# A new order of the first loads, pair 0 scaled on one engine, and two moved instructions in a fused attention and mixer kernel

## The chip, the cores and the metric

The kernel runs on one core of one Trainium2 chip. A core has five engines, each with its own queue of instructions that it works off in order: TensorE (PE in the profile) for matrix products, VectorE (DVE), ScalarE (ACT), GpSimd (POOL), and SyncE (SP), which here only issues DMA transfers. Engines wait for one another through semaphores. The metric is the time of one execution on the device in microseconds (us); lower is better.

## The reference

Two stages follow one another. The first is cosine attention over 8 batches and 12 heads, sequence 448, head size 64:

```
q_n = q / (norm(q) + 1e-06);  k_n = k / (norm(k) + 1e-06)
attn = softmax(q_n @ k_n.T / tau)          # tau = 0.1
x = attn @ v                               # heads side by side: (8, 448, 768)
```

The second is an MLP mixer on x, without normalisation:

```
h = maximum(x.T @ w_tok1, 0) @ w_tok2      # w_tok1 448x256, w_tok2 256x448
u = x + h.T
out = u + maximum(u @ w_ch1, 0) @ w_ch2    # w_ch1 768x1536, w_ch2 1536x768
```

Inputs and output are 32-bit floats. The kernel multiplies in 16-bit floats.

## The kernel before, in words

The heads are taken in pairs: 6 pairs in each of 8 batches, 48 in all. The sequence of 448 is split into 4 chunks of 112 rows. One pair passes through these steps:

- `load`: three DMA copies (q, k, v; 224 KB each) from SyncE. There are five buffers of each, so that pair i + 5 is loaded while pair i is at work.
- `squares` (GpSimd; ScalarE for pairs 0 and 1), `norm_sum` (VectorE), `norm_root` (ScalarE: logarithm, then exponential of half of it), `norm_rec` (VectorE): they give one over the norm.
- `normalize`: q and k are multiplied by it and written in 16 bits. GpSimd does it, except that for pair 0 VectorE takes half of k.
- `tpose_pe`: eight TensorE transposes and a copy out of PSUM by VectorE (for pair 0 by ScalarE, q and k apart). From pair 14 on a DMA transposes instead.
- `score`: TensorE, four tiles of 112x896, with two PSUM buffers between them; `expo`: ScalarE takes the exponential of each.
- `v_cast`: V is cast to 16 bits, by ScalarE or VectorE, as a list of pairs says.
- `pv`: 32 matmuls give output and row sums; VectorE divides and writes x.

Everything runs in an order written out by hand; no scheduler moves anything. `opening(i)` issues the instructions of slots 0 to 12, `slot(i)` those of the later ones. In slot i the scores of pair i, the output of pair i - 1 and the preparation of pairs i + 1 to i + 3 stand side by side. `fill()` puts in matmuls of the mixer of an earlier batch, from slot 7 on (`spread` sets how many).

The mixer of batch 0 starts inside the opening slots. In slots 2 to 6 it goes pair by pair: `tok1_pair` (first token weight, TensorE, then a relu on ScalarE), `tok2_pair` (second token weight), and `u_pair`, an addition on VectorE done twice: once into 16 bits, from which a DMA transposes a piece of uT, and once into 32 bits. Slot 6 handles two pairs, 4 and 5, and so has four additions.

The weights of the token stage come in 32 bits: `w1_load` (seven pieces and one repeated piece) and `w2_load` on SyncE. VectorE casts w1 in slot 1 (`w1_cast`, two halves of a 128x1280 tile); ScalarE casts w2 in slots 1 and 2 (`w2_cast`). The last 64 rows of w1 are kept twice, once in partitions 0 to 63 with zeros beside them, and once in partitions 64 to 127 (fifth column block), for batches with an odd number. The channel weights come through GpSimd's queue in slots 1, 3, 5, 7 and 9 to 11 (`wc1_job`, `wc2_job`).

The order of the first loads on SyncE (lines 439 to 452) is: q, k of pair 0; q, k of pair 1; v of 0; q, k of 2; v of 1; q, k of 3; w1; w2; q, k of 4; v of 2, 3, 4.

Of the kernel before, what the change touches and what calls it, by code (L numbers as in the profile page):

```python
# [9 lines left out]
FP32 = mybir.dt.float32  # L10
FP16 = mybir.dt.float16
AF = mybir.ActivationFunctionType
ALU = mybir.AluOpType
# [5 lines left out]
def _bcast_free(ap: bass.AP, n: int) -> bass.AP:  # L19
    return bass.AP(tensor=ap.tensor, offset=ap.offset, ap=list(ap.ap) + [[0, n]])  # L20
# [3 lines left out]
def kernel(  # L24
# [19 lines left out]
    nc = tc.nc  # L44

    B, H, S, E = q.shape
# [51 lines left out]
    def ident():  # L98
        nc.gpsimd.memset(id16[:], 0.0)
        nc.gpsimd.affine_select(out=id16[:], in_=id16[:], compare_op=ALU.not_equal,  # L100
                                fill=1.0, base=0, pattern=[[-1, 128]], channel_multiplier=1)
        for t in v16s:
            nc.gpsimd.memset(t[:, :, E:E + 1], 1.0)
        st = mix.tile([128, 5, T], FP32, name="w1s", tag="u32", bufs=2)
        stage["w1"] = st
        nc.gpsimd.memset(st[64:128, 3, :], 0.0)
        nc.gpsimd.memset(st[0:64, 4, :], 0.0)

    def w1_load(n):
        st = stage["w1"]  # L110
        rows = moe_w_tok1.rearrange("(p c) t -> c p t", c=NCH)
        if n < 3:
            for f, m in f_segments(128 * n, 128 * n + 128):
                c, p = f // P, f % P
                nc.sync.dma_start(out=st[f - 128 * n:f - 128 * n + m, n, :],
                                  in_=rows[c, p:p + m, :])
        else:
            nc.sync.dma_start(out=st[0:64, 3, :], in_=rows[3, P - 64:P, :])
            nc.sync.dma_start(out=st[64:128, 4, :], in_=rows[3, P - 64:P, :])

    def w2_load():
        st = mix.tile([128, TT, S], FP32, name="w2s", tag="u32", bufs=2)
# [3 lines left out]
    def recast(out, in_):  # L126

        nc.vector.tensor_reduce(out=out, in_=bass.AP(tensor=in_.tensor, offset=in_.offset,  # L128
                                                     ap=list(in_.ap) + [[1, 1]]),
                                axis=AXX.X, op=ALU.max)  # L130

    def w1_cast(z):
        a, o = (t[:].rearrange("p n t -> p (n t)") for t in (stage["w1"], w1t))
        h = 5 * T // 2
        recast(o[:, z * h:(z + 1) * h], a[:, z * h:(z + 1) * h])

    def w2_cast(tt):
        nc.scalar.copy(out=w2t[:, tt, :].rearrange("k (c p) -> k c p", c=NCH),
# [21 lines left out]
    def load(i, names="qkv"):  # L160
        b, pj = pairs[i]
        for nm in names:
            t = ld.tile([P, 2, NCH, E], FP32, name=f"{nm}l", tag=f"{nm}l")
            nc.sync.dma_start(
                out=t[:].rearrange("p g c e -> p g (c e)"),
                in_=src[nm][b, 2 * pj:2 * pj + 2].rearrange("g (p c) e -> p g (c e)", c=NCH))
            st_[i][nm] = t

    def squares(i, act=""):
        s = st_[i]  # L170
        s["sq"] = att.tile([P, 2, 2 * NCH, E], FP32, name="sq", tag="sq", bufs=2)
        for j, nm in enumerate("qk"):
            a = s[nm][:].rearrange("p g c e -> p (g c) e")
            if nm in act:
                nc.scalar.activation(out=s["sq"][:, j], in_=a, func=AF.Square)  # L175
            else:
                nc.gpsimd.tensor_mul(out=s["sq"][:, j], in0=a, in1=a)  # L177

    def small(i, nm):
        if nm not in st_[i]:  # L180
            st_[i][nm] = att.tile([P, 2, 2 * NCH], FP32, name=nm, tag=nm)
        return st_[i][nm]
# [3 lines left out]
    def norm_sum(i, j=BOTH):  # L186
        nc.vector.tensor_reduce(out=small(i, "ssq")[:, j], in_=st_[i]["sq"][:, j], axis=AXX.X,  # L187
                                op=ALU.add)

    def norm_root(i, j=BOTH):  # L190
        nc.scalar.activation(out=small(i, "ln")[:, j], in_=small(i, "ssq")[:, j], func=AF.Ln)  # L191
        nc.scalar.activation(out=nns[i % 3][:, j, :, 0], in_=small(i, "ln")[:, j], func=AF.Exp,
                             scale=0.5)

    def norm_rec(i, j=BOTH):

        nc.vector.tensor_reduce(out=small(i, "nre")[:, j], in_=nns[i % 3][:, j], axis=AXX.X,
                                op=ALU.add)
        nc.vector.reciprocal(out=small(i, "rn")[:, j], in_=small(i, "nre")[:, j])  # L199

    def normalize(i, vec):
        s = st_[i]
        t = att.tile([P, 2, NCH, 2, E], FP16, name="qkn", tag="qkn")
        for j, nm in enumerate("qk"):
            for g in ((0, 1) if vec and j else (BOTH,)):
                eng = nc.vector if g == 1 else nc.gpsimd
                rn = small(i, "rn")[:, j].rearrange("p (g c) -> p g c", g=2)[:, g]
                o = t[:, j, :, g, :]
                if g == BOTH:
                    o = o.rearrange("p c g e -> p g c e")  # L210
                eng.tensor_tensor(out=o, in0=s[nm][:, g], in1=_bcast_free(rn, E), op=ALU.mult)  # L211
        s["qkn"] = t

    def v_cast(i, act):
# [47 lines left out]
    def expo(i, c):  # L262
        s = st_[i]
        nc.scalar.activation(out=s["p"][:, c], in_=s["pS"][c][:, :, 0:S], func=AF.Exp,  # L264
                             scale=inv_tau)
# [174 lines left out]
    eps()  # L440
    load(1, "qk")
    ident()
    load(0, "v")
    load(2, "qk")
    load(1, "v")
    load(3, "qk")
    for n in range(4):
        w1_load(n)
    w2_load()
    load(4, "qk")  # L450
    for n in (2, 3, 4):
        load(n, "v")
    squares(0, act="qk")
    for j in range(2):
        norm_sum(0, j)
        norm_root(0, j)
    for j in range(2):
        norm_rec(0, j)
    squares(1, act="qk")
    normalize(0, True)  # L460
    tpose_pe(0, act=True)
    norm_sum(1)
    norm_root(1)
    norm_rec(1)
    squares(2)

    wide = {**{i: partial(wc1_job, n) for n, i in enumerate((1, 3, 5, 7))},
# [1 line left out]

    def opening(i):  # L470

        normalize(i + 1, False)
        score(i, 0)
        norm_sum(i + 2)
        expo(i, 0)
        expo(i, 1)
        if not i:
            v_cast(0, True)
        norm_root(i + 2)
        v_cast(i + 1, i in (0, 2, 3, 4, 5))  # L480
        squares(i + 3)
        if i in wide:
            wide[i]()
        fill()
        if i >= 1:
            pv(i - 1, 0)
            pv(i - 1, 1)
        norm_rec(i + 2)
        if i in (1, 2):
            w2_cast(i - 1)  # L490
        r_, u_, add = first[0] if first else (None,) * 3
        done = [i - 2] if 2 <= i <= NPAIR else []
        if done:
            r_(i - 2)
        fill()
        score(i, 1)
        expo(i, 2)
        expo(i, 3)
        tpose_pe(i + 1)
        if i == NPAIR:  # L500
            r_(i - 1)
            done.append(i - 1)
        for pj in done:
            u_(pj)
        for half in (True, False):
            for pj in done:
                add(pj, half)
        if i == 1:
            w1_cast(0)
            w1_cast(1)  # L510
        fill()
        fill()
        fill()
# [98 lines left out]
```

## Time and profile before

| | before |
|---|---|
| median of 3 runs | 413.39 us (412.63 to 414.4) |
| the profiled execution | 413.88 us |
| its span, first to last instruction | 411.5 us |
| TensorE busy | 383.9 us, 93% of the span |
| VectorE busy | 233.9 us, 57% |
| ScalarE busy | 262.1 us, 64% |
| GpSimd busy | 198.2 us, 48% |
| moved by DMA | 63.63 MB, mean 155 GB/s |

The span lies 2.4 us below the profiled execution's own time; that rest lies outside the first and last instruction. Times below are from the start of the span. The profile shows, for each engine, when an instruction started, how long it took, and what ended the idle time before it; a chain of waits, followed back from the last instruction; and the clock granted to TensorE, as a share of its full speed.

### The profile page before, as it was taken

The numbers are of one execution on the slowest core, as the hardware profiler recorded it, in microseconds if no ns is written. First come the engines' busy times: TensorE is split into PE (matmuls) and PEld (weight loads), VectorE is DVE, ScalarE is ACT, GpSimd is POOL, SyncE is SP. The second block draws the span as 40 slices with busy tenths as digits, with TensorE's granted clock in tenths as the row PEclk, the third lists the DMA queues.
The fourth block names the chain that finished last, engine by engine and source line by source line (L and its number), as shares of the span: only waits on it lengthen the run. The fifth ranks groups of instructions, "written<-read, shape, count | busy, mean of one in ns | idle before, by whom it ended". The sixth has DMA issues, their size and how long they took to land.

```text
span 411.5 us, 9002 instructions
## 1 busy us (share of the span) xinstructions
PE 383.9 (93%) x3592; PEld 220.6 (54%) x3592; DVE 233.9 (57%) x530; ACT 262.1 (64%) x452; POOL 198.2 (48%) x207
## 2 busy tenths in 40 slices
PE   2768789899999999999999999999999999999996
PEld 1456556556445556555545556555545556655453
DVE  4499978748634776548643676448643683152022
ACT  6879869876576666765677666775677665522400
POOL 4979969934743564634653464635563430000000
PEclk9989989999999999999999999999999999999999
DMA  8899999966974588649876488539963253027013
GB/s 212 239 247 216 221 252 234 248 139 140 238 155 109 139 181 198 160 75 184 219 178 150 124 196 198 151 84 199 209 166 91 61 120 101 2 43 149 0 43 112
DMA packets 97385, 63.63 MB, mean 155 GB/s; under 512 B 57536, under 2 KB 93888, under 8 KB 97344
## 3 DMA queue, kind: packets, MB, share of 16 engines
q1 hardware_dynamic: 94032, 58.20, 60.1%
q0 software_dynamic: 3184, 4.72, 6.7%
q8 instruction: 28, 0.46, 0.5%
q10 hardware_dynamic: 128, 0.15, 0.1%
q14 instruction: 13, 0.11, 0.1%
HBM read 43.45 MB, written 11.01 MB: 132 GB/s over the span
## 4 chain that ended last, share of the span: by engine, by line
PE 78%; DVE 11%; DMA 3%; ACT 3%; POOL 2%; issue 1%; DVEq 0%; POOLq 0%
PE pG L375 27%; PE pF L384 25%; PE pO L278 9%; PE pS L257 9%; PE pR L309 5%; PE pU L322 3%; DVE ssq L187 2%; DVE x L285 2%; ACT pE L264 2%; DMA uT<-u 1%; DVE qkT L246 1%; DMA kl<-in_k_dram 1%; POOL qkn L211 1%; DVE u L366 1%; DVE u L331 1%; POOL sq L177 1%
## 5 line engine op out<-in xcount | busy, mean ns | idle before, releaser
L264 ACT ACTIVATE pE<-pS 112x896 f16<-112x896 f32 x192 | 164.9, 914 | 39.5 <-PE pS L257 38.8
L375 PE MATMUL pG<-uT,wc1t 128*128 128x384 f16 (+1 forms) x576 | 121.4, 355 | 0.3 <-DMA uT<-u 0.3
L384 PE MATMUL pF<-wc2t,gT 128*128 128x384 f16 x672 | 116.6, 326 | 0.2
L211 POOL TENSOR_TENSOR qkn<-ql,rn 112x512 f16<-112x512 f32 x48 | 50.1, 1044 | 137.7 <-DVE rn L199 122.4
L384 PEld LDWEIGHTS <-gT 128*128 128x128 f16 x672 | 63.6, 98 | 47.0 <-issue 7.3
L377 ACT ACTIVATE gT<-pG 128x384 f16<-128x384 f32 (+1 forms) x96 | 52.6, 548 | 45.9 <-PE pG L375 45.1
L375 PEld LDWEIGHTS <-wc1t 128*128 128x128 f16 x576 | 51.7, 98 | 51.9 <-issue 11.5
L388 DVE TENSOR_TENSOR u<-pF,u 128x384 f32<-128x384 f32 x56 | 31.1, 556 | 78.5 <-PE pF L384 78.0
L257 PE MATMUL pS<-qkT 64*112 64x448 f16 x384 | 60.2, 384 | 13.2 <-DVE qkT L246 10.3
L278 PEld LDWEIGHTS <-pE 112*128 112x128 f16 x1536 | 60.8, 100 | 15.9 <-issue 5.4
L278 PE MATMUL pO<-v,pE 112*128 112x65 f16 x1536 | 64.8, 196 | 0.0
L187 DVE TENSOR_REDUCE ssq<-sq 112x16 f32<-112x1024 f32 (+1 forms) x49 | 58.3, 1192 | 5.5 <-ACT sq L175 3.7
L284 DVE RECIPROCAL rec<-pO 128x6 f32<-128x6 f32 x96 | 17.5, 182 | 77.1 <-PE pO L278 76.1
L211 POOL TENSOR_TENSOR qkn<-kl,rn 112x512 f16<-112x512 f32 (+1 forms) x48 | 49.8, 1038 | 0.0
L177 POOL TENSOR_TENSOR sq<-ql 112x512 f32<-112x512 f32 x46 | 48.8, 1061 | 1.6 <-ACT qkT L244 1.2
L177 POOL TENSOR_TENSOR sq<-kl 112x512 f32<-112x512 f32 x46 | 48.5, 1053 | 0.2 <-DMA kl<-in_k_dram 0.2
L285 DVE TENSOR_TENSOR x<-pO,rec 128x384 f16<-128x384 f32 x96 | 40.9, 426 | 3.3
L257 PEld LDWEIGHTS <-qkT 64*112 64x112 f16 x384 | 19.0, 127 | 39.1 <-issue 22.8
L128 DVE TENSOR_REDUCE v<-vl 112x512 f16<-112x512 f32 x39 | 24.9, 639 | 3.4 <-DMA vl<-in_v_dram 3.4
L331 DVE TENSOR_TENSOR u<-pU,x 128x384 f32<-128x384 f32 x50 | 25.4, 545 | 0.1
L337 ACT CAST u<-u 128x768 f16<-128x768 f32 x14 | 11.6, 832 | 20.9 <-DVE u L331 20.9
L191 ACT ACTIVATE ln<-ssq 112x16 f32<-112x16 f32 (+1 forms) x49 | 10.9, 223 | 17.7 <-DVE ssq L187 17.5
(41 smaller groups left out, 181.9 us busy)
## 6 DMA issues: line engine op xcount, KB each, us to landing
ql<-in_q_dram SPq DMA_DIRECT2D x48, 224.0 KB, 3.8
kl<-in_k_dram SPq DMA_DIRECT2D x48, 224.0 KB, 4.0
vl<-in_v_dram SPq DMA_DIRECT2D x48, 224.0 KB, 4.2
out_dram<-u SPq DMA_DIRECT2D x8, 336.0 KB, 3.5
wc1t<-in_moe_w_ch_dram POOLq DMA_DIRECT2D x4, 576.0 KB, 7.5
wc2t<-in_moe_w_ch_dram POOLq DMA_DIRECT2D x3, 768.0 KB, 10.3
out_dram<-u SPq DMA_DIRECT2D x8, 288.0 KB, 3.8
out_dram<-u SPq DMA_DIRECT2D x7, 240.0 KB, 3.1
```

The costliest lines, as they stand in the source:

```text
L177: nc.gpsimd.tensor_mul(out=s["sq"][:, j], in0=a, in1=a)
L187: nc.vector.tensor_reduce(out=small(i, "ssq")[:, j], in_=st_[i]["sq"][:, j], axis=AXX.X, op=ALU.add)
L211: eng.tensor_tensor(out=o, in0=s[nm][:, g], in1=_bcast_free(rn, E), op=ALU.mult)
L257: nc.tensor.matmul(pS[:, h, 0:S], s["T"][64 * h:64 * h + 64, 1, c * P:(c + 1) * P], s["T"][64 * h:64 * h + 64, 0, :], start=True, stop=True)
L264: nc.scalar.activation(out=s["p"][:, c], in_=s["pS"][c][:, :, 0:S], func=AF.Exp, scale=inv_tau)
L278: nc.tensor.matmul(pO[:, n, h, :], s["p"][:, c, h, c0:c0 + 128], s["v16"][:, NCH * h + c, 0:E + 1], start=(c == 0), stop=(c == NCH - 1))
L285: nc.vector.tensor_tensor(out=xt[hp:hp + nr, t0:t0 + len(ts), d0:d0 + 2 * E].rearrange("p t (h e) -> p t h e", h=2), in0=pO[m0:128, :, :, ...
L331: nc.vector.tensor_tensor(out=u32[:, i - t0, cols], in0=pU[:], in1=xt[:, i, cols], op=ALU.add)
L375: nc.tensor.matmul(pG[:], wc1t[:, dt, ct * 128:(ct + 1) * 128], uT[:, dt, :], start=(dt == 0), stop=(dt == DT - 1))
L377: nc.scalar.activation(out=gT[:, ct, :], in_=pG[:], func=AF.Relu)
L384: nc.tensor.matmul(pF[:], gT[:, ct, (i - t0) * 128:(i - t0 + 1) * 128], wc2t[:, ct, dh * DH:(dh + 1) * DH], start=(ct == 0), stop=(ct == C ...
L388: nc.vector.tensor_tensor(out=o, in0=pF[:], in1=o, op=ALU.add)
```

## The change

- The first loads are issued in another order: q, k of pairs 0, 1, 2; v of 0; q, k of 3; v of 1 and 2; q, k of 4; w1; w2; v of 3 and 4.
- The repeated piece of w1 isn't loaded any more. The zeros are written by GpSimd into the 16-bit tile, VectorE casts 768 columns of 128 partitions and 256 columns of 64 partitions in slot 1, and in slot 8 copies the 16-bit rows from partitions 0 to 63 to partitions 64 to 127.
- Pair 0 is scaled on VectorE alone, q and k whole.
- Pair 1: q is squared on ScalarE, k on GpSimd, and the norms are summed in two halves. Its root and its reciprocal are issued in slot 0 after the first exponential, and its scaling after these.
- The 32-bit addition of pair 5 is issued in slot 7, after the copy of pair 8's transposes, not in slot 6.
- V of pair 8 is cast in slot 7 by ScalarE, not by VectorE.

```
@@ ident
-        st = mix.tile([128, 5, T], FP32, name="w1s", tag="u32", bufs=2)
+        st = mix.tile([128, 4, T], FP32, name="w1s", tag="u32", bufs=2)
         stage["w1"] = st
-        nc.gpsimd.memset(st[64:128, 3, :], 0.0)
-        nc.gpsimd.memset(st[0:64, 4, :], 0.0)
+        nc.gpsimd.memset(w1t[64:128, 3, :], 0.0)
+        nc.gpsimd.memset(w1t[0:64, 4, :], 0.0)
@@ w1_load
             nc.sync.dma_start(out=st[0:64, 3, :], in_=rows[3, P - 64:P, :])
-            nc.sync.dma_start(out=st[64:128, 4, :], in_=rows[3, P - 64:P, :])
@@ w1_cast
-        a, o = (t[:].rearrange("p n t -> p (n t)") for t in (stage["w1"], w1t))
-        h = 5 * T // 2
-        recast(o[:, z * h:(z + 1) * h], a[:, z * h:(z + 1) * h])
+        if z < 2:
+            p, n = (slice(0, 64), slice(3, 4)) if z else (slice(0, 128), slice(0, 3))
+            recast(w1t[p, n, :], stage["w1"][p, n, :])
+        else:
+            recast(w1t[64:128, 4, :], w1t[0:64, 3, :])
@@ normalize
-            for g in ((0, 1) if vec and j else (BOTH,)):
-                eng = nc.vector if g == 1 else nc.gpsimd
...
+            eng = nc.vector if vec else nc.gpsimd
+            rn = small(i, "rn")[:, j].rearrange("p (g c) -> p g c", g=2)
+            eng.tensor_tensor(out=t[:, j].rearrange("p c g e -> p g c e"), in0=s[nm][:],
+                              in1=_bcast_free(rn, E), op=ALU.mult)
@@ the first loads and steps
     load(1, "qk")
     ident()
+    load(2, "qk")
     load(0, "v")
-    load(2, "qk")
+    load(3, "qk")
     load(1, "v")
-    load(3, "qk")
+    load(2, "v")
+    load(4, "qk")
     for n in range(4):
         w1_load(n)
     w2_load()
-    load(4, "qk")
-    for n in (2, 3, 4):
-        load(n, "v")
+    load(3, "v")
+    load(4, "v")
...
-    squares(1, act="qk")
+    squares(1, act="q", names="q")
+    squares(1, names="k")
     normalize(0, True)
     tpose_pe(0, act=True)
-    norm_sum(1)
-    norm_root(1)
-    norm_rec(1)
+    for j in range(2):
+        norm_sum(1, j)
     squares(2)
@@ opening
-        normalize(i + 1, False)
-        score(i, 0)
-        norm_sum(i + 2)
-        expo(i, 0)
+        if i:
+            normalize(i + 1, False)
+            score(i, 0)
+            norm_sum(i + 2)
+            expo(i, 0)
+        else:
+            score(0, 0)
+            expo(0, 0)
+            norm_root(1)
+            norm_rec(1)
+            normalize(1, False)
+            norm_sum(2)
         expo(i, 1)
...
-        v_cast(i + 1, i in (0, 2, 3, 4, 5))
+        v_cast(i + 1, i in (0, 2, 3, 4, 5, 7))
...
         for pj in done:
             u_(pj)
+        if i == NPAIR + 1:
+            first[0][2](NPAIR - 1, False)
         for half in (True, False):
             for pj in done:
-                add(pj, half)
+                if half or pj != NPAIR - 1:
+                    add(pj, half)
+        if i == NPAIR + 2:
+            w1_cast(2)
```

More of the change, by code (lines that the diff above doesn't have):

```diff
@@ L167, in load, with squares @@
             st_[i][nm] = t
-    def squares(i, act=""):
+    def squares(i, act="", names="qk"):
         s = st_[i]
-        s["sq"] = att.tile([P, 2, 2 * NCH, E], FP32, name="sq", tag="sq", bufs=2)
-        for j, nm in enumerate("qk"):
+        if "sq" not in s:
+            s["sq"] = att.tile([P, 2, 2 * NCH, E], FP32, name="sq", tag="sq", bufs=2)
+        for nm in names:
+            j = "qk".index(nm)
             a = s[nm][:].rearrange("p g c e -> p (g c) e")
@@ L204, in normalize @@
         for j, nm in enumerate("qk"):
-            for g in ((0, 1) if vec and j else (BOTH,)):
-                eng = nc.vector if g == 1 else nc.gpsimd
[L207 to L211, printed above, removed]
+            eng = nc.vector if vec else nc.gpsimd
+            rn = small(i, "rn")[:, j].rearrange("p (g c) -> p g c", g=2)
+            eng.tensor_tensor(out=t[:, j].rearrange("p c g e -> p g c e"), in0=s[nm][:],
+                              in1=_bcast_free(rn, E), op=ALU.mult)
         s["qkn"] = t
```

## The prediction

> **What bounds the kernel now.** I read the page's slices first, then the chain of waits, then each engine in order of time over the first 62 us, where the diff acts, and the clock.
>
> ```profile
> PE   2768789899999999999999999999999999999996
> DVE  4499978748634776548643676448643683152022
> PEclk9989989999999999999999999999999999999999
> ...
> PE 78%; DVE 11%; DMA 3%; ACT 3%; POOL 2%; issue 1%; DVEq 0%; POOLq 0%
> ```
>
> A slice is 10.3 us. TensorE (PE) is full from slice 9 on, so there a microsecond is only won by starting earlier. In the first eight slices it isn't full, and the granted clock dips in slices 3 and 6. The order of instructions on TensorE is the same in both kernels, so time won before 60 us should reach the end nearly whole. What holds it up early:
>
> ```profile
> 15.01 1.22 DVE L187 TENSOR_REDUCE ssq<-sq 112x16 f32<-112x1024 f32 x1 [0.75 <-POOL sq L177]
> 19.62 0.69 DVE L128 TENSOR_REDUCE v<-vl 112x512 f16<-112x512 f32 x1 [3.39 <-DMA vl<-in_v_dram]
> ...
> 22.07 0.62 DVE L246 COPY qkT<-pT 128x896 f16<-128x896 f16 x1
> ```
>
> ```profile
> 22.75 0.99 PE L257 MATMUL pS<-qkT 64*112 64x448 f16 x4 [3.56 <-DVE qkT L246]
> ...
> 53.60 2.10 PE L375 MATMUL pG<-uT,wc1t 128*128 128x384 f16 x6
> ```
>
> (Start, us taken, engine, line, operation, and the idle time before it.) VectorE (DVE) waits 3.4 us for V of pair 2; the copy of pair 2's transposes is queued behind that, and TensorE then stands 3.6 us. The second place is slot 7: VectorE runs without a gap to 52.9, TensorE idles 2.65 us for pair 8's copy, and the six matmuls after that take 2.1 us, against 1.14 at 58.04. The clock says why:
>
> ```profile
> 19.15:22.56 3.41, 0.04 (x1) 1.00 1.12 270
> 22.56:25.97 3.41, 3.22 (x42) 0.50 1.13 256
> 25.97:29.39 3.42, 2.49 (x27) 1.00 1.12 257
> ...
> 49.86:53.28 3.42, 0.77 (x12) 1.00 0.93 203
> 53.28:56.69 3.41, 3.41 (x32) 0.50 1.11 226
> ```
>
> (Stretch, TensorE busy us, clock.) After a stretch of 3.41 us with 0.04 or 0.77 us of work, the next 3.41 us have half the clock; after 2.49 us it stays full. At the very start the column reads 1.00, but four score matmuls take 0.99 us until 22.75 and 0.59 from 26.22: TensorE runs at half pace there too.
>
> **The loads.** The first ten loads run in one file: k of pair 0 lands at 4.1, q1 6.2, k1 7.1, the tenth (k of pair 3) 7.2 us after its issue at 5.18, so at 12.4. From the third to the tenth that is 0.89 us each. SP's eleventh issue, at 6.18, is at the landing of the third copy: each waits for the one eight before it. In the new order pair 2's q and k are fifth and sixth (7.9, 8.8), V of pair 0 9.7, V of pair 1 tenth (12.4), V of pair 2 eleventh (13.3, not 19.6), pair 4's k thirteenth (15.1; before, issue 14.04 plus 4.5 = 18.5). VectorE's 3.4 us wait goes.
>
> What is late next is the channel weight w2. It becomes the twenty-first issue and waits for the thirteenth landing, 15.1. Before it took
>
> ```profile
> w2s<-in_moe_w_tok_dram SPq DMA_DIRECT2D x1, 448.0 KB, 3.6
> ```
>
> so it lands at 18.7 (before 12.9 + 3.6 = 16.5). w1 is in by about 16.5 (its last part issues at 14.2 and takes 2.1 to 2.4) and is wanted near 19.5. ScalarE (ACT) casts w2 in slot 1 ahead of two exponentials.
>
> **Slot 0.** Before, GpSimd scales q in 5.97 to 7.01 and half of k to 7.76, VectorE the other half:
>
> ```profile
> 5.97 1.04 POOL L211 TENSOR_TENSOR qkn<-ql,rn 112x512 f16<-112x512 f32 x1 [3.73 <-DVE rn L199]
> 6.97 0.79 POOL L211 TENSOR_TENSOR qkn<-kl,rn 112x256 f16<-112x256 f32 x1
> ```
>
> VectorE's half (256 elements) ran 6.46 to 7.29, 0.83 us; only 0.28 of it lies after GpSimd's q. GpSimd's half took 0.79, not half of 1.04. I read both as one waiting for the other: 0.28 us for 256 elements, some 0.6 for 512. (128x384 products elsewhere take 0.56, which gives 0.75 as upper end without a wait; 2 x 0.83 = 1.67 if the wait were its own pace.) New: q 6.46 to 7.06, k to 7.66, scores at 8.85, not 9.0: 0.15 gained. But GpSimd now squares pair 1's k, which lands at 7.06, just when VectorE goes from q to k. If GpSimd slips in between, k is 1.04 later. I take it that VectorE keeps on.
>
> The Trainium skill, "SBUF — State Buffer", section "🔬 SBUF: two separate sides", says that a GpSimd operation and a VectorE operation with two SBUF inputs exclude each other for the whole instruction; that agrees with the pair of rows, and it speaks against this change, as it puts a GpSimd square among the VectorE products: with GpSimd in between, the sum below would be about 0.5 less.
>
> Pair 1's root now stands behind the first exponential, 9.5 to 10.4 on ScalarE, so its reciprocal is ready at 11.3, not 9.98; GpSimd was busy squaring pair 2 until 10.98 anyway, so its scaling moves from 10.94 to 11.3. All of slot 0 behind that is 0.3 us later: pair 2's root, V of pair 1, exponentials, pair 3's root, w2 cast at 17.25, not 16.96.
>
> **Slots 1 and 2.** ScalarE waits 17.25 to 18.7, casts (0.98), pair 1's last exponentials end at 21.3 (before 19.7). VectorE meanwhile casts V of pair 2 at 16.6, does pair 0's output (17.2 to 18.5), the reciprocal, and pair 2's copy at 19.5, not 22.07. The w1 casts shrink from 2 x 640 columns (22.61 to 24.07, 1.14 ns a column) to 768 + 256: 1.17 for 1.46, 0.3 gained. So pair 2's exponentials start on ScalarE at 21.3, not 23.41: 2.1; the train behind them (root, V cast, second w2 cast, relu) reaches its last exponentials at 25.05, not 27.36: 2.3; and VectorE's next block, which waits for them, comes at 28.0, not 30.43: **2.4 us**. Pair 5's loads for that stretch land about where they did (w2 2.2 later, but V of 2 and q, k of 4 no longer in between). From there to slot 6 ScalarE and VectorE repeat unchanged at 4.44 us a slot.
>
> Bounds: if w2 takes 2.1 us, the quickest weight copy, ScalarE doesn't wait and VectorE sets 3.0; if 6.6, the slowest (w1's first), ScalarE waits 4.45 and the 2.4 becomes -0.6. I take 3.6, its own row. If the clock is halved through slot 2 (TensorE is idle from about 19.5 to 21.7 but for two matmul pairs), the scores, transposes and pU there take about twice as long and the gain is 1.3.
>
> **Slots 6 to 8.** Slot 6 loses one of four additions (0.47) and slot 7 the V cast (0.59) ahead of pair 8's copy: it ends at 51.85 in old time, not 52.91. **1.06 us**, TensorE's idle time falls from 2.65 to 1.6. ScalarE takes the cast (0.6) after pair 9's root, which comes 0.47 earlier; its last exponential ends near 52.1, just before the scores need it. The addition returns behind pair 8's copy (0.5), ahead of a 2.36 us idle: nothing, and with a full clock VectorE would still be free at 54.05 for an output at 54.3. The pieces for the six matmuls land at 52.3 (issue 49.0 + 3.3), just ahead of 52.5. Slot 8 gains a 64x256 cast, 0.29 + 0.06; pair 10's copy has 0.34 of idle before it: nothing, at most 0.35. The two GpSimd memsets (0.3 each) only change their target.
>
> If TensorE's shorter pause no longer halves the clock, the six matmuls take 1.14 (1.0 less) and the 32 after them 1.19, not 1.69: **1.5 us** more. Its busy share would be about half a stretch; the rows show 0.23 tripping and 0.73 not. Unknown between, and where the stretch falls is chance. The Trainium skill, "TensorE: Matmul & The Clock Gate", section "🔬 Part 1: The HAM clock gate (the "warmup" mystery)", asks for a whole idle window; by it both pauses are too short and the sum would be 5.0, though this trace shows 0.77 us of work not sufficing.
>
> **Sum.** One of the two slow stretches stays, the other goes: 2.4 + 1.06 = 3.5 (slot 8 slow), or 1.3 + 1.06 + 1.5 = 3.9 (slot 2 slow). I take 3.6. The profiled execution took 413.88 (span 411.5 and 2.4 around it), 0.5 above the median 413.39: 410.3 beside the profile, 409.8 beside the median; I say **410.0**.
>
> **Rivals.**
> - Both slow stretches go: 2.4 + 1.06 + 1.5 = 5.0, 408.4 to 408.9. For: both pauses are shorter than those that tripped. Against: at the start busy shares of 0.66 (12.32 to 15.73) and 0.73 (8.91 to 12.32) did not bring the full pace.
> - Both stay, or GpSimd slips in (1.04, of which ScalarE's wait for w2 hides about half): 1.3 + 1.06 = 2.4, less 0.5: 1.9 to 2.4, 411.0 to 411.5.
> - The wait for w2 takes the place of that for V: each late microsecond past 18.7 costs one. At a landing of 20.5 or later the early gain is under 0.6 and the whole 0.6 to 1.7: about 412.3. For: six small w1 pieces ahead of it each hold one of eight places. Against: it only waits for the thirteenth landing.
> - Slower than before: the same wait at its upper bound. With w2 at 21.7 the sum is -0.6 + 1.06 = +0.5; past 22.2 it turns to a loss, past 24.3 the loss exceeds 0.5%, 415.5.
>
> **Chances.** 0.42, 0.22, 0.22, 0.10, 0.04 in that order. 0.5% (2.07 us) is about what can be told from no change: faster means under 411.3, so the first two, half the third: 0.75; the rest of the third and the fourth, 0.21, same; 0.04 slower. The range runs from 407.8 (both stretches gone, 408.4, and the 0.6 that an early w2 adds) to 412.4 (w2 in V's place); it leaves out about 0.15.
>
> **What would show it.** V's wait of 3.4 gone on VectorE; ScalarE idle about 1.5 us before the first w2 cast; VectorE's two scalings of about 0.6 each, scores at 8.85; the output block of slot 3 at about 28; one halved stretch, not two; TensorE's pause before pair 8's scores about 1.6. I am wrong if w2 lands after 20, if both stretches stay, or if TensorE waits later for something that the earlier start doesn't bring forward (a transposed piece, a load).

## The result and the profile after

The changed kernel takes 410.59 us (median of 16 executions), the kernel before 413.37 (median of 16 beside it). The ratio is 0.9926, 95% interval 0.9909 to 0.9943: 0.74% faster. The profiled execution took 411.94 us with a span of 410.1 us; before it was 413.88 with 411.5. So of the 1.94 us between the two profiled executions 1.4 lie in the span and 0.54 outside it. One of the 16 executions, 416.08 us at a mean clock of 0.982, lies over 1.5% above the fastest and isn't in the ratio; with it the changed kernel's mean is 411.07 us, without it 410.74.

The page of the changed kernel, its slices and the shares of its chain:

```profile
PE   1779789889999999999999999999999999999996
DVE  5688998648534766558644766548643673152022
PEclk9978999999999999999999999999999999999999
...
PE 77%; DVE 9%; DMA 6%; POOL 4%; issue 1%; ACT 1%; SPq 1%; DVEq 0%; POOLq 0%
```

TensorE is as full from slice 10 on as before; slice 9 fell from 9 to 8, and the third wait below lies in it. The clock dips once, in slices 3 and 4, and no longer in slice 6. VectorE's part of the chain fell and that of DMA doubled. The two places that the prediction started from, VectorE first and TensorE after it (start, us, engine, line, operation, idle time before it):

```profile
16.75 1.22 DVE L190 TENSOR_REDUCE ssq<-sq 112x16 f32<-112x1024 f32 x1 [0.75 <-POOL sq L180]
17.89 0.68 DVE L127 TENSOR_REDUCE v<-vl 112x512 f16<-112x512 f32 x1
...
20.37 0.62 DVE L246 COPY qkT<-pT 128x896 f16<-128x896 f16 x1
```

```profile
21.05 0.69 PE L257 MATMUL pS<-qkT 64*112 64x448 f16 x4 [0.77 <-DVE qkT L246]
...
52.02 0.63 PE L257 MATMUL pS<-qkT 64*112 64x448 f16 x4 [1.59 <-DVE qkT L246]
52.58 1.15 PE L375 MATMUL pG<-uT,wc1t 128*128 128x384 f16 x6
```

V of pair 2 is cast without a wait. TensorE's pauses fell from 3.56 to 0.77 us and from 2.65 to 1.59, and the six matmuls in slot 8 run at full pace (1.15, not 2.10). But the ends do not add up so simply. Three things came in between.

First, slot 0 is later than before. VectorE scales pair 0, GpSimd squares pair 1's k:

```profile
6.84 0.64 DVE L210 TENSOR_TENSOR qkn<-ql,rn 112x512 f16<-112x512 f32 x1
7.40 1.53 DVE L210 TENSOR_TENSOR qkn<-kl,rn 112x512 f16<-112x512 f32 x1
```

```profile
7.17 1.21 POOL L180 TENSOR_TENSOR sq<-kl 112x512 f32<-112x512 f32 x1 [4.94 <-DMA kl<-in_k_dram]
8.34 1.48 POOL L180 TENSOR_TENSOR sq<-ql 112x512 f32<-112x512 f32 x1
```

The k scaling takes 1.53 us against 0.64 for q of the same size, and the GpSimd squares around it 1.21 and 1.48 against 1.04 elsewhere. GpSimd's first square started at 7.17, ahead of VectorE's k scaling at 7.40, and VectorE finished after it; the second square, at 8.34, finished after VectorE. Pair 1's copy starts at 15.37, before at 13.63.

Second, a half-clock stretch now comes in slot 3. In stretches of 3.41 us (length, TensorE busy us with the number of matmuls, clock, then two columns on DMA):

```profile
22.88:26.29 3.41, 1.95 (x26) 1.00 1.13 255
26.29:29.70 3.41, 3.13 (x39) 0.52 1.18 234
29.70:33.12 3.42, 3.34 (x28) 0.50 1.10 160
...
50.18:53.59 3.41, 1.82 (x16) 1.00 1.09 237
53.59:57.01 3.42, 3.15 (x51) 1.00 1.11 227
```

It lasts two lengths. Ahead of the first change on record the column can't be read: it says 1.00 from the start, but matmuls of known size show the pace. In the changed kernel four score matmuls take 0.94 us at 18.85 and eight transposes 0.57 at 19.72 (0.93 at 18.26 in the kernel before), so TensorE came to its full pace at about 19.5 and lost it again at 26.3. In the kernel before it ran at half pace until 26.0, apart from a stretch at 19.15 to 22.56 with hardly any work.

VectorE's output block (the reciprocals and products that write x) is 2.0 us ahead of before in slot 2 (23.23 against 25.22), 1.2 in slot 3 (29.23 against 30.43) and 0.1 behind in slot 4 (35.01 against 34.88): in this execution nothing of the early gain is left there. The late edits then bring 2.4 us (54.53 against 56.97 in slot 8).

Third, TensorE has a wait that wasn't there before:

```profile
75.61 0.58 PE L257 MATMUL pS<-qkT 64*112 64x448 f16 x4 [1.05 <-DVE qkT L246]
85.63 0.58 PE L257 MATMUL pS<-qkT 64*112 64x448 f16 x4 [1.18 <-DMA qkT<-qkn]
```

At 75.61 it is 2.4 us ahead (before 77.99), at 85.63 only 1.1 (before 86.76, no wait). Pair 14 is the first that a DMA transposes. The issue came 2.4 us earlier (77.12 against 79.50), but took 8.5 us to land, not 6.1: it landed at 85.6 in both kernels.

Executions of one program differ by 2 to 6 us, and in these two kernels the mean granted clock goes with it. Over the executions of before beside the experiments below (84), and those of the changed kernel that its ratio uses (15):

| mean granted clock | before: executions, mean us | changed: executions, mean us |
|---|---|---|
| up to 0.990 | 34, 414.60 | 1, 411.94 |
| 0.991 to 0.997 | 39, 413.23 | 5, 411.32 |
| 0.998 and more | 11, 412.14 | 9, 410.28 |
| all | 84, 413.64 (clock 0.9907) | 15, 410.74 (clock 0.9961) |
| time outside the span, median | 2.41 | 1.84 |

The means differ by 2.90 (2.57 with the execution of 416.08). Between executions of 0.998 and more the difference is 1.86, 0.57 of it outside the span; so about 1.3 us is time won on the path, 0.6 lies outside the span, and the last 1.0 goes with halved stretches that are on record less often in the changed kernel. This is an estimate: the mean clock counts no half pace ahead of the first change on record, so that 0.998 doesn't mean full pace from the start.

### The profile page after: what moved, and what is told of

Its sections match the earlier page's. It is cut to its first block, busy times and chain, and to the rows that moved or that the text cites. A ratio compares the mean times of both kernels' runs of the same rounds, so it can differ in the third digit from the quotient of the medians.

```text
span 410.1 us, 8998 instructions
## 1 busy us (share of the span) xinstructions
PE 383.2 (93%) x3592; PEld 220.5 (54%) x3592; DVE 234.5 (57%) x532; ACT 261.6 (64%) x452; POOL 197.8 (48%) x206
## 4 chain that ended last, share of the span: by engine, by line
PE 77%; DVE 9%; DMA 6%; POOL 4%; issue 1%; ACT 1%; SPq 1%; DVEq 0%; POOLq 0%
PE pF L384 26%; PE pG L375 25%; PE pO L278 9%; PE pS L257 9%; PE pR L309 4%; PE pU L322 3%; DMA kl<-in_k_dram 3%; DMA qkT<-qkn 2%; POOL qkn L210 2%; DVE ssq L190 2%; POOL sq L180 2%; DVE x L285 1%; DMA ql<-in_q_dram 1%; DVE u L366 1%; DVE u L331 1%
## 5 line engine op out<-in xcount | busy, mean ns | idle before, releaser
L210 POOL TENSOR_TENSOR qkn<-ql,rn 112x512 f16<-112x512 f32 x47 | 49.0, 1043 | 133.4 <-DVE rn L202 110.8
L180 POOL TENSOR_TENSOR sq<-kl 112x512 f32<-112x512 f32 x47 | 49.6, 1054 | 4.9 <-DMA kl<-in_k_dram 4.9
L210 POOL TENSOR_TENSOR qkn<-kl,rn 112x512 f16<-112x512 f32 x47 | 49.0, 1042 | 0.0
```

Of the source, the lines that this page charges most:

```text
L210: eng.tensor_tensor(out=t[:, j].rearrange("p c g e -> p g c e"), in0=s[nm][:], in1=_bcast_free(rn, E), op=ALU.mult)
```

## The experiments

Ratios are against the kernel before on the same chip, with 95% intervals. "Mean" is over the executions compared.

| kernel | ratio (95%) | mean us | mean clock | outside the span |
|---|---|---|---|---|
| changed kernel | 0.9926 (0.9909 to 0.9943) | 410.74 | 0.9961 | 1.84 |
| e1 loads only | 0.9985 (0.9962 to 1.0009) | 413.08 | 0.9897 | 2.44 |
| e2 late edits only | 0.9977 (0.9953 to 1.0000) | 412.64 | 0.9932 | 2.47 |
| e3 pair 1's k squared on ScalarE | 0.9924 (0.9895 to 0.9952) | 410.05 | 0.9975 | 1.87 |
| e4 a third of the second channel weight left out | 0.9937 (0.9914 to 0.9959) | 410.44 | 0.9965 | 1.87 |
| e5 w1 edit only | 0.9991 (0.9972 to 1.0010) | 413.22 | 0.9910 | 2.47 |
| e6 pair 0 edit only | 1.0005 (0.9978 to 1.0032) | 413.79 | 0.9922 | 1.95 |
| e7 all but the pair 0 edit | 0.9944 (0.9920 to 0.9968) | 411.55 | 0.9957 | 2.46 |
| e8 e3, pair 14 on TensorE | 0.9929 (0.9906 to 0.9952) | 410.68 | 0.9955 | 1.99 |
| e9 before, pause filled | 0.9979 (0.9961 to 0.9998) | 412.62 | 0.9957 | 2.44 |
| e10 e3, w2 ahead of pair 4 | 0.9912 (0.9886 to 0.9938) | 409.77 | 0.9949 | 1.85 |
| e11 e10, pair 14 on TensorE | 0.9917 (0.9887 to 0.9947) | 410.25 | 0.9943 | 1.88 |
| e12 e10, pause filled | 0.9885 (0.9858 to 0.9911) | 408.73 | 0.9993 | 1.88 |

The four parts by themselves (e1, e2, e5, e6) give 0.15, 0.23, 0.09 and -0.05%, together 0.42% against 0.74% for the whole. Each of these is uncertain by 0.2 to 0.3%, so whether the parts help one another isn't shown.

**The load order alone.** The kernel before with the first loads in the new order:

```
     load(1, "qk")
     ident()
+    load(2, "qk")
     load(0, "v")
-    load(2, "qk")
+    load(3, "qk")
     load(1, "v")
-    load(3, "qk")
+    load(2, "v")
+    load(4, "qk")
     for n in range(4):
         w1_load(n)
     w2_load()
-    load(4, "qk")
-    for n in (2, 3, 4):
-        load(n, "v")
+    load(3, "v")
+    load(4, "v")
```

> The kernel before with only the new order of the first loads (w1 still in eight pieces, the repeated one included). Theory: the load order is the early gain, and the change's own slot 0 took part of it back. Here VectorE's 3.4 us wait for V of pair 2 goes, slot 0 keeps its old times (scores at 9.0), ScalarE reaches the w2 cast at 17.0 and waits for it until about 19.5 (one piece more ahead of w2), pair 2's copy comes near 19 and the output block of slot 3 near 28. Without the late edits TensorE's pause of 2.65 us in slot 7 stays. Total: 1.0 to 2.0 us faster than before. Rival: what the early part wins is lost again by slot 4 whatever sets slot 0, since TensorE's clock halves after the shorter pauses too (as in the profile of the changed kernel): within 0.5 us of before.

It is 0.15% faster with an interval that includes no change: less than the theory's 1 to 2 us. Its ScalarE:

```profile
16.64 0.22 ACT L192 ACTIVATE nn<-ln 112x16 f32<-112x16 f32 x1
19.39 0.99 ACT L138 CAST w2t<-w2s 128x448 f16<-128x448 f32 x1 [2.53 <-DMA w2s<-in_moe_w_tok_dram]
```

With slot 0 as before ScalarE is at the w2 cast by 16.9 and waits 2.5 us. The wait for V of pair 2 is replaced, on another engine, by one three quarters as long. Slot 2's output block comes at 24.15, 1.1 us ahead of before, but slot 4's at 34.38, only 0.5 ahead. TensorE's pace took part of this. The clock column reads 1.00 from 18 to 51 us, but the matmuls run at half pace until 27.9, two microseconds longer than in the kernel before:

```profile
22.61 1.94 PE L278 MATMUL pO<-v,pE 112*128 112x65 f16 x32
27.91 0.58 PE L257 MATMUL pS<-qkT 64*112 64x448 f16 x4
```

VectorE waits for them, 1.71 us for the output of slot 2 and 1.25 for the transposes of pair 3. TensorE's 2.65 us pause in slot 7 is still there, and in the profiled execution the clock is halved after it from 51.9 to 58.7. So the result lies nearer the rival's (within 0.5 us; 0.65 by the means) than the theory's 1 to 2, though TensorE didn't drop after the shorter pause: it hadn't come to its full pace yet. The wait for w2 and this pace both took of the gain.

**The late edits alone.** The kernel before with these two:

```
-        v_cast(i + 1, i in (0, 2, 3, 4, 5))
+        v_cast(i + 1, i in (0, 2, 3, 4, 5, 7))
...
+        if i == NPAIR + 1:
+            first[0][2](NPAIR - 1, False)
         for half in (True, False):
             for pj in done:
-                add(pj, half)
+                if half or pj != NPAIR - 1:
+                    add(pj, half)
```

> The kernel before with only the two late edits: the 32-bit addition of pair 5 in slot 7 and V of pair 8 cast on ScalarE. Theory: pair 8's copy ends 1.0 us earlier, TensorE's pause falls from 2.65 to about 1.6 us, the half-clock stretch after it goes, so that at 57 us VectorE is 2.4 us ahead; pair 14's transposed piece still lands at about 85.6, so 1.2 us of it is lost in a wait of TensorE there: 1.0 to 1.5 us faster than before. Rival one: nothing caps it, 2.2 to 2.6 us faster. Rival two: the half-clock stretch stays in this kernel, 0.5 to 1.0 us faster.

The means differ by 1.1 us (413.73 before in that series), the ratio says 0.95: the low end of the theory, with an interval that ends at no change. Pair 8's copy starts 5.00 us after pair 7's (50.67 and 45.67); before it was 6.07 (52.27 and 46.20). TensorE's pause is 1.59, the stretch after it isn't halved, and pair 14's transposed piece lands 7.7 us after its issue at 76.4, at 84.1, where TensorE waits 0.43 us.

**GpSimd's square in between.** The changed kernel with:

```
-    squares(1, act="q", names="q")
-    squares(1, names="k")
+    squares(1, act="qk")
```

> The changed kernel with one thing undone: pair 1's k is squared on ScalarE again, not on GpSimd. Theory: the 1.53 us of VectorE's k scaling of pair 0 was GpSimd's square in between; here it takes 0.65, GpSimd's squares of pair 2 take 1.04 each, scores start at about 9.2, not 10.16, and slot 0 ends about 1 us earlier. ScalarE then reaches the w2 cast about 1 us before the copy lands (18.7) and waits there, so that slot 2 is only 0 to 0.5 us earlier; total 0 to 0.7 us faster than the changed kernel. Rival: k scaling has a pace of its own (its first row of before, 0.83 for half): then it stays at 1.5 us and nothing changes.

VectorE's scalings in this kernel:

```profile
6.80 0.64 DVE L210 TENSOR_TENSOR qkn<-ql,rn 112x512 f16<-112x512 f32 x1
7.36 0.69 DVE L210 TENSOR_TENSOR qkn<-kl,rn 112x512 f16<-112x512 f32 x1
```

With GpSimd's square elsewhere the k scaling takes 0.69 us, so its 1.53 was the square, not a pace of its own; the rival falls. Scores start at 9.28, not 10.16. ScalarE's w2 cast is at 17.80 without a wait here; w2 was issued at 14.0 and in by 17.6. In the eighth experiment, with the same start, it was in at 19.0 and ScalarE waited 1.26. The mean is 0.7 us under the changed kernel's, but the intervals overlap widely, and the clock was fuller (0.9975).

**The backlog of transfers.** The changed kernel with:

```
-            **{i: partial(wc2_job, n) for n, i in enumerate((9, 10, 11))}}
+            **{i: partial(wc2_job, n) for n, i in enumerate((9, 10))}}
...
-                                     wc2t[:, ct, dh * DH:(dh + 1) * DH],
+                                     wc2t[:, ct % 8, dh * DH:(dh + 1) * DH],
```

> The changed kernel without the third load of the second channel weight (768 KB in slot 11); the last four of its twelve blocks are multiplied with blocks 8 earlier, so that part of the product is computed with other rows of the weight. TensorE's work is the same. Theory: pair 14's transposed piece stands behind a backlog of transfers, which is why it lands at 85.6 in both kernels; 768 KB less (about 2.9 us at 270 GB/s) lets it land by about 83, TensorE's 1.2 us wait for it goes, and the total is 1.0 to 2.0 us faster than the changed kernel. Rival: the transposition itself is slow after the switch from TensorE's, and the backlog doesn't matter: no change beyond 0.3 us (GpSimd saves one issue of 0.8 us).

The transposed pieces of pairs 14 and 15 land in 4.5 us or less after their issue, the first issued at 75.42, and the wait is gone: the chain of this kernel runs on TensorE alone from 74.93 to 130 (start, us, engine, tile, line, count):

```profile
78.30 0.52 PE pS L257 x4
78.81 1.08 PE pG L375 x6
79.90 1.30 PE pR L309 x8
81.20 0.26 PE pO L278 x8
81.45 1.30 PE pR L309 x8
82.76 0.52 PE pS L257 x4
```

So the lateness is a backlog behind other transfers, not the transposition. In time it is less clear than expected: executions of 0.998 and more average 409.43 (4 of them) against 410.28 (9) for the changed kernel, 0.85 us less, but the means over all executions differ by only 0.3, and the intervals of the two ratios overlap almost wholly. The theory's 1 to 2 us were not found.

**The w1 edit alone**, in the kernel before:

```
-        st = mix.tile([128, 5, T], FP32, name="w1s", tag="u32", bufs=2)
+        st = mix.tile([128, 4, T], FP32, name="w1s", tag="u32", bufs=2)
...
-        nc.gpsimd.memset(st[64:128, 3, :], 0.0)
-        nc.gpsimd.memset(st[0:64, 4, :], 0.0)
+        nc.gpsimd.memset(w1t[64:128, 3, :], 0.0)
+        nc.gpsimd.memset(w1t[0:64, 4, :], 0.0)
...
-            nc.sync.dma_start(out=st[64:128, 4, :], in_=rows[3, P - 64:P, :])
...
-        a, o = (t[:].rearrange("p n t -> p (n t)") for t in (stage["w1"], w1t))
-        h = 5 * T // 2
-        recast(o[:, z * h:(z + 1) * h], a[:, z * h:(z + 1) * h])
+        if z < 2:
+            p, n = (slice(0, 64), slice(3, 4)) if z else (slice(0, 128), slice(0, 3))
+            recast(w1t[p, n, :], stage["w1"][p, n, :])
+        else:
+            recast(w1t[64:128, 4, :], w1t[0:64, 3, :])
...
+        if i == NPAIR + 2:
+            w1_cast(2)
```

> The kernel before with only the edit of w1: the repeated piece isn't loaded, zeros go into the 16-bit tile, VectorE casts 768 and 256 columns and copies the rows up in slot 8. The executions so far leave 2.45 us outside the span for before and for the first two experiments, and 1.86 us for the changed kernel and its two variants. Theory: one transfer less shifts which of eight places each later transfer takes, and the 0.6 us at the end comes with it: here too 1.8 to 1.9 us lie outside the span, and the time is 0.6 to 0.9 us under before. Rival: it comes from the pair 0 edit (the start), then 2.45 us stay here and the time is that of before, within 0.4.

No difference that can be told, and 2.47 us outside the span: the theory that one transfer less brings the 0.6 us there falls.

**The pair 0 edit alone**, in the kernel before:

```
-            for g in ((0, 1) if vec and j else (BOTH,)):
-                eng = nc.vector if g == 1 else nc.gpsimd
+            eng = nc.vector if vec else nc.gpsimd
...
-    squares(1, act="qk")
+    squares(1, act="q", names="q")
+    squares(1, names="k")
...
-    norm_root(1)
-    norm_rec(1)
...
+            score(0, 0)
+            expo(0, 0)
+            norm_root(1)
+            norm_rec(1)
+            normalize(1, False)
+            norm_sum(2)
```

> The kernel before with only the edit of slot 0: pair 0 scaled on VectorE, pair 1's k squared on GpSimd, pair 1's root after the first exponential. Theory: GpSimd's square slips between VectorE's two scalings, k takes 1.5 us, pair 1's copy moves from 13.6 to about 15.4, and the wait for V of pair 2 until 19.6 still hides all of it: within 0.5 us of before. Rival: it costs what it delays, 1 to 1.7 us slower.

No change in time: the wait for V hides slot 0, as the theory says. But in its profiled execution the k scaling took 0.68 us: here VectorE kept on, and GpSimd's square took 1.52. Which goes first follows from which starts first: here VectorE's k scaling at 7.33, GpSimd's square at 7.39; in the changed kernel and in e4 the square (7.17 and 7.33) ahead of the scaling (7.40 and 7.47). GpSimd starts when pair 1's k has landed, so a tenth or two in a load decides it. The time outside the span is 1.95 here. The 0.5 us there comes with this edit: all kernels with it have 1.84 to 1.99, all without 2.41 to 2.47. It isn't pair 1's square, which e3, e8 and e10 to e12 have on ScalarE; the scaling of pair 0 and the later root of pair 1 weren't told apart. Why isn't settled.

**All but the pair 0 edit.** The changed kernel with the lines of the sixth experiment taken back:

```
-            eng = nc.vector if vec else nc.gpsimd
+            for g in ((0, 1) if vec and j else (BOTH,)):
+                eng = nc.vector if g == 1 else nc.gpsimd
...
-    squares(1, act="q", names="q")
-    squares(1, names="k")
+    squares(1, act="qk")
...
-            score(0, 0)
-            expo(0, 0)
-            norm_root(1)
-            norm_rec(1)
-            normalize(1, False)
-            norm_sum(2)
...
+    norm_root(1)
+    norm_rec(1)
```

> The changed kernel with the whole edit of slot 0 undone. Theory: slot 0 is 1.7 us earlier (pair 1's copy at 13.6), ScalarE waits 1.5 to 2 us for w2 at 18.7, pair 2's copy comes at 19 to 19.5, and slot 2 is 0 to 0.7 us earlier than in the changed kernel; pair 14's transposed piece takes most of that back: total 0 to 0.7 us faster than the changed kernel. Rival: the longer wait for w2 is a pause of TensorE that halves its clock more often, and this is 0.5 to 1.5 us slower than the changed kernel.

ScalarE waits 2.50 us for w2, which lands at 20.2. The mean is 411.55, 0.8 over the changed kernel's; 0.6 of that is the time outside the span, so within the span the pair 0 edit is worth 0.2, no more than the uncertainty. The theory had the sign wrong and the rival's range (0.5 to 1.5 slower) holds the number, but not for its reason: the mean clock (0.9957) is that of the changed kernel.

**Pair 14 on TensorE.** The third experiment with one more opening slot:

```
-    FIRST = 2 * NPAIR + 1
+    FIRST = 2 * NPAIR + 2
```

> The changed kernel with pair 1's k squared on ScalarE (as in the third experiment), and one more slot in the form of the first thirteen, so that pair 14 is transposed on TensorE and copied by VectorE, not by a DMA. Theory: TensorE's wait of about 1 us for pair 14's piece goes, its transposes cost 0.6 us: 0.2 to 0.8 us faster than the third experiment. Rival: the next piece, pair 15's, is as late and takes the wait over: no change or slower by the 0.6 us of transposes.

TensorE waits for no transposed piece (pair 15's lands 3.1 us after its issue at 83.46), but the time is no better than the third experiment's: 410.68 against 410.05. Executions of 0.998 and more are 0.4 faster (409.1 against 409.5, three each), which isn't enough to tell. The theory isn't confirmed; the rival's number fits, but not its reason, since pair 15's piece isn't late.

**The pause filled, in the kernel before.**

```
         tpose_pe(i + 1)
+        if i == NPAIR + 1:
+            pD = ps.tile([128, 128], FP32, name="pD", tag="ps")
+            for _ in range(24):
+                nc.tensor.matmul(pD[:], id16[:], id16[:], start=True, stop=True)
```

> The kernel before, with 24 matmuls of the identity by itself into a PSUM tile that nobody reads, put after pair 8's transposes in slot 7, where TensorE idles 2.65 us; nothing else. Theory: the half-clock stretch after that pause is what makes executions of before differ and is most of what the late edits save. The matmuls take 1.4 to 2.6 us of the pause, TensorE's busy share there rises above three quarters, the stretch at 53 goes, the mean granted clock rises from 0.990 to 0.994 or more and the mean time falls by 0.8 to 1.5 us. Rival: the clock is a by-product and the path runs elsewhere: within 0.4 us of before.

Nothing else is changed, and no result of these matmuls is used. TensorE in slots 7 and 8:

```profile
49.94 1.50 PE L503 MATMUL pD<-id 128*128 128x128 f16 x24
52.75 0.59 PE L257 MATMUL pS<-qkT 64*112 64x448 f16 x4 [1.30 <-DVE qkT L246]
53.27 1.15 PE L375 MATMUL pG<-uT,wc1t 128*128 128x384 f16 x6
54.25 1.18 PE L278 MATMUL pO<-v,pE 112*128 112x65 f16 x32
```

The matmuls after the pause run at full pace, though pair 8's copy is as late as before. The kernel is 0.21% faster (0.02 to 0.39%), 0.7 us in the mean of that series, and its mean clock is 0.9957, not 0.992. So the halved clock after a pause is a cost of its own: more work on TensorE made the kernel faster, though by an interval that only just leaves out no change. It is the low end of what was expected, and about half of the 1.5 us that the profile before shows for the stretch; where the rest went isn't shown. The mean clock of an execution doesn't tell it here: the six executions of 0.998 and more average 412.66 us, the other six 412.58, and the profiled one (411.8) has a halved stretch from 21.0 to 27.8 us.

**w2 ahead of pair 4.** The third experiment with:

```
-    load(4, "qk")
     for n in range(4):
         w1_load(n)
     w2_load()
+    load(4, "qk")
     load(3, "v")
```

> The third experiment (changed kernel, pair 1's k squared on ScalarE) with w1 and w2 loaded ahead of pair 4's q and k. Theory: w2 lands at about 17 and ScalarE doesn't wait for it (1.3 to 2.5 us in the kernels with a short slot 0); pair 4's q and k land by about 19.5, when GpSimd gets to them; slot 2 comes about 1 us earlier than in the third experiment; pair 14's transposed piece takes part of it: 0.2 to 0.8 us faster than the third experiment's 409.75. Rival: GpSimd now waits for pair 4, which gives the gain back: same as the third experiment within 0.3.

ScalarE reaches the w2 cast at 17.61 and doesn't wait, as it didn't in the third experiment's profile. Slot 2's output block is at 22.51 (23.00 in the third experiment, whose scores began 0.2 later). Most of this is TensorE's pace, not w2: here it is full by 20.3 us (32 output matmuls take 1.19 at 20.86), in the third experiment at about 24.5, and the next two experiments, which load w2 as early but run at half pace until 24.6 or later, have the block at 22.99 and 22.91. In the tenth's profiled execution the clock was halved twice, 26.6 to 30.0 and 50.5 to 54. The mean, 409.77, is 0.3 under the third experiment's: the theory's sign, not told apart from no change.

**The same with pair 14 on TensorE** (the edit of the eighth experiment on the tenth):

```
-    FIRST = 2 * NPAIR + 1
+    FIRST = 2 * NPAIR + 2
```

> The tenth experiment with one more opening slot, so that pair 14 is transposed on TensorE. Theory: a microsecond won early is taken by the wait for pair 14's transposed piece; without that wait the early gain goes through: 0.5 to 1.2 us faster than the tenth experiment. Rival: as in the eighth experiment, no gain over the same kernel without it (within 0.4), because the slot in this form costs what the wait did.

No gain over the tenth: 410.25 against 409.77, 0.5 slower and not told apart from no change. One reason may be what its profile shows: TensorE, now early in slot 8, waits 0.72 and 0.24 us for a transposed piece of the mixer, and the clock was halved again in slot 8.

**The same with the pause filled** (the edit of the ninth experiment on the tenth):

```
+        if i == NPAIR + 1:
+            pD = ps.tile([128, 128], FP32, name="pD", tag="ps")
+            for _ in range(24):
+                nc.tensor.matmul(pD[:], id16[:], id16[:], start=True, stop=True)
```

> The tenth experiment with the 24 identity matmuls after pair 8's transposes. Theory: the pause there is down to 1.6 us and the halved stretch occurs only in part of the executions; filling it helps less than in the kernel before, 0 to 0.5 us in the mean, with a mean granted clock of 0.998 or more and a narrower spread. Rival: the extra matmuls delay pair 8's scores (the pause holds 1.6 us, they take 1.4 to 2.6): 0.2 to 1.0 us slower.

The spread of the two, run side by side:

| | executions | mean clock | times, us |
|---|---|---|---|
| tenth | 11 | 0.9949 | 407.98 to 413.55 |
| with the pause filled | 6 | 0.9993 | 408.20 to 410.22 |

It has the lowest mean of all: 0.9885 of before (0.9858 to 0.9911), 1.15% faster, and 1.0 us under the tenth, more than the theory gave it, though with so few executions, and the tenth's spread of 5.6 us, that 1.0 isn't clear of noise. In the profiled execution no halved stretch is on record between 18 and 60 us, but TensorE still runs at half pace until about 24.7 (the first two lines). Pair 8's scores start 0.18 us after the fill:

```profile
21.37 1.95 PE L278 MATMUL pO<-v,pE 112*128 112x65 f16 x32
24.90 0.57 PE L238 MATMUL pT<-id,qkn 112*128 112x112 f16 x8
...
49.55 0.63 PE L257 MATMUL pS<-qkT 64*112 64x448 f16 x4 [0.18 <-DVE qkT L246]
50.11 0.99 PE L375 MATMUL pG<-uT,wc1t 128*128 128x384 f16 x5
51.33 0.32 PE L375 MATMUL pG<-uT,wc1t 128*128 128x384 f16 x1 [0.23 <-DMA uT<-u]
```

Against the changed kernel the intervals just touch (0.9911 and 0.9909), and the two were not run side by side; the means are 2.0 us apart.

## Why the prediction was right

The forecast was 410.0 us, faster, with 407.8 to 412.4; measured 410.59. Sign and size hold. The steps did less well than their sum, and part of that is luck.

- *The loads.* VectorE's wait for V is gone. w2 was reckoned to land at 18.7 and landed 3.5 us after its issue at 15.19, at 18.7. To the tenth that is luck: in other kernels with this order and as many pieces it was issued between 14.0 (e3) and 16.5 (e7) and landed between 17.6 and 20.2. (The text calls w2 the channel weight; it is the second token weight. The sum doesn't depend on it.)
- *Slot 0.* The side taken ("VectorE keeps on") was the wrong one for the profiled execution. Scores at 10.16, not 8.85; of these 1.3 us, 0.4 is a later start of VectorE's scalings (6.84 against 6.46). The price given for the other side, 1.04, is near what the third experiment shows (k scaling 0.69 against 1.53, scores 0.9 earlier). The sixth, with the same slot 0 in the kernel before, shows the side taken.
- *ScalarE's wait for w2, 1.45 us.* It didn't occur in the profiled execution, since the late slot 0 brought ScalarE there at 18.70, just as the piece landed. The first, seventh and eighth experiments show it (2.53, 2.50, 1.26 us): the step was right that w2 is late next, and slot 0 and w2 are two prices of which only the larger is paid.
- *The early gain, 2.4 or 1.3 us.* Too large at 2.4. In the changed kernel's profile it is 1.2 in slot 3 and gone in slot 4, by a halved stretch of two lengths; in e4, the same program up to slot 10 without that stretch, it is 1.55 in slots 3 and 4 (28.88 and 33.33 against 30.43 and 34.88), with TensorE at half pace until about 25 us. That is near the 1.3 given for a slot 2 at half pace. The 2.4 needs the full pace in slots 2 and 3, and none of the 14 profiles shows it: either TensorE comes to the full pace only at 24 to 28 us (e1, e3 to e6, e8, e11, e12), or it is there by about 20 and drops again at 21 to 27 (before, the changed kernel, e2, e7, e9, e10). The load order by itself gave 0.65 us in the means, not told apart from none. The term was mis-sized by about one microsecond.
- *The late edits, 1.06 us and 1.5 for the clock.* Right: pair 8's copy is 1.07 nearer to pair 7's, the pause 1.59 as computed, the stretch gone in this profile, 2.4 us together at slot 8. That the stretch would stay in some executions was right too: the three profiles with the full 2.65 us pause besides before's (e1, e5, e6) have it after that pause; of the eight with 1.58 or 1.59 left unfilled five (the changed kernel, e2, e3, e4, e7) don't, and three (e8, e10, e11) do; the two with the pause filled don't.
- *One of two stretches stays.* So it was in the profiled execution, but it moved to slot 3 and lasted two lengths. In 9 of the 15 executions none can be on record (0.998 and more; one stretch alone takes 0.004), against 11 of 84 before.
- *"Time won before 60 us should reach the end nearly whole."* This failed. 1.2 us went into the wait for pair 14's transposed piece, which a backlog of transfers holds (e4). The text had named a transposed piece among what would make it wrong, but no term was set for it.
- *What lies around the span* was taken as fixed at 2.4. It fell by 0.57, which came with the pair 0 edit (e5 to e7). Nothing in the prediction covers it.

For the two profiled executions: 0 from slots 0 to 4, 2.4 from slots 6 to 8, 1.2 lost at pair 14, 0.2 to 0.3 won behind (before's 0.30 us wait for a transposed piece at 108 us is gone), 0.54 outside: 1.94. So the sum of 3.6 had about 1 us too much in the early term and no term for the 1.2 lost at pair 14. The median still came to 2.8 because 0.57 outside the span, which had no term, and fewer halved stretches than the one reckoned with made up for part of both; that is luck.

The Trainium skill's "SBUF — State Buffer", section "🔬 SBUF: two separate sides", on exclusion between GpSimd and a VectorE operation with two SBUF inputs, is borne out by the 1.53, 1.21 and 1.48 us rows and by the third experiment. Its "TensorE: Matmul & The Clock Gate", section "🔬 Part 1: The HAM clock gate (the "warmup" mystery)", asks for a whole idle window before the clock drops; here a stretch with 1.95 of 3.41 us busy preceded a drop, and the measurement decides.

## What to carry to other kernels

When a wait is removed, list what is late next on every engine, the DMA queues included, down to the point where the engine that bounds the kernel is full: here three waits (the second weight, GpSimd's square, a transposed piece) each took a microsecond of the same gain, and they overlap, so that only the largest of those side by side is paid. A pause of the matrix engine can cost more than itself, through the clock after it; filling it with matmuls that nobody needs can pay (0.21% in the kernel before, 0.02 to 0.39%). With effects of half a percent, look at the clock of every execution before reading two profiles against each other, and check the clock column by the duration of a matmul that you know: it read 1.00 where 32 matmuls took 1.94 us, not 1.19.

## What was not expected of the hardware

- The clock was halved after a stretch of 3.41 us with 1.95 us of TensorE work (22.88 to 26.29, changed kernel) and not after one with 1.82 us (50.18 to 53.59, same execution). Nor did 3.13 us of work in the halved stretch from 26.29 bring the full pace back, where 3.22 us did in the kernel before (22.56 to 25.97). Busy time as the trace has it doesn't settle the drop; what does stays open.
- Ahead of the first change on record the clock reads 1.00 though matmuls run at half pace, until 27.9 us in e1 and 24.7 in e12.
- 24 unused matmuls in a pause of 2.65 us made the kernel before 0.21% faster (0.02 to 0.39%).
- Two engines' square and scaling of 112x512 elements, 0.64 to 0.69 and 1.04 us apart from each other, take 1.53 and 1.48 when they meet. The one that starts first goes first, by 0.14 to 0.23 us for GpSimd (changed kernel, e4), by 0.06 for VectorE (e6).
- About half a microsecond outside the span (2.41 to 1.84) goes with the pair 0 edit, with or without pair 1's square on GpSimd. No run explains it.
